# Attention in plain float32 with the two heads of a pair on halves of the TensorE array, instead of a split into high and low parts

## The chip, the cores and the metric

The kernel runs on one core of one Trainium2 chip. The metric is the device time of the program in microseconds (us); the times shown are of separate executions, and one further execution was taken with the hardware profiler. All rows and windows below are of that profiled execution, and times in them count from its first instruction.

## The reference, cut to what matters

Two parts, in float32. First an attention with a memory term, for 4 batches, 8 heads, 576 positions and 64 dimensions per head:

```
scores = q @ k.T / 8, causal mask
a      = softmax(scores)
local  = a @ v
phi(x) = x + 1 where x > 0, else exp(x)
mem    = (phi(q) @ M_prev) / (phi(q) @ z_prev + 1e-6)
out    = g * mem + (1 - g) * local        with g = sigmoid(beta) per head
```

Then a feed-forward on the 2304 rows of 512 that this gives: `h = x @ w_in` (512 to 2048), `r = relu(h)`, `y = (s * r * r + b) @ w_out` (2048 to 512).

## The kernel before, in words

**Pairs.** The 32 heads are worked in 16 pairs; a pair holds two heads of one batch side by side on the 128 partitions (64 dimensions each). Pairs 0 to 3 are batch 0 (`g < NP` in the code). A head's 576 query rows are cut into five tiles: one of 64 and four of 128 (`QS`, `QW`); tile i sees the keys 0 to `QW[i]`, so its scores are 64, 192, 320, 448 and 576 columns wide, the last one in two halves of 288.

**F32R and its split.** TensorE takes a plain float32 matmul as two MATMUL instructions (two passes), each of which streams its columns at half the speed of an F32R pass. F32R keeps fewer bits of its operands, so the kernel writes a number as a high part H (a rounded copy, made by ScalarE) and a low part L (the rest, made by a subtraction on VectorE or GpSimd) and sums several F32R products. The feed-forward does so everywhere (lines L482 to L484 for the first product `mm1`, L745 to L747 for the second).

**Scores.** For pairs 1 to 15 the q and k of a pair are split (`split_qk`, cast L235, subtractions L232 into tile `sqk`) and stacked by four DMAs per pair (`stack_qk`, L269) into `X`, in which a head's high and low parts lie one above the other on 128 partitions. `s_mm` then does two F32R passes per score tile and head (L300, L301). Pair 0 alone takes plain float32 on its 64 partitions (L295). Each tile is masked, scaled and its row minimum taken out of PSUM by one VectorE instruction (`s_red`, L314), then exponentiated with row sums by ScalarE (`s_exp`, L322). `s_norm` makes the reciprocal of the five row sums (L329, L330) and scales the five probability tiles (L334, most on GpSimd), once per head.

**Transposes and the second product.** The probabilities of a head are transposed in 15 blocks by TensorE (`pt_bank`, L373; ten of 128 x 128, four of 128 queries by the first 64 keys, one of 64 by 64) into PSUM banks and copied out by ScalarE. phi(q), scaled by g over its norm (`phi_a` to `phi_c`, L201 to L217), is transposed on its own, two heads at once in five blocks (`t_phi`, L252). For pairs 0 to 3 everything is then multiplied in plain float32 for one head at a time: `av_mm32` with phi by M_prev (L405) and the first 64 keys (L406) on 64 partitions each, and the other keys on 128 (L408). For pairs 4 to 15 (`own`) the transposed probabilities and phi are split as well (`evac`: cast L221, subtraction out of PSUM L225), V is split (`split_v`, L287, L288), the phi parts are stacked by DMA (`stack_qp`), and `av_mm` does F32R passes (L420 to L424) whose output is 128 wide: one half from V's high part, the other from its low part; `av_evac` adds the two (L439, L440). At the end `x_split` splits the pair's output into `xs` (L451 on GpSimd, L452), the operand of `mm1`.

**Order.** Every step has a position in a list `EV` (pair n starts at 2n, head x at x). The list is sorted and run; with it the feed-forward's weights are loaded, converted from 64-bit words and split at positions `WT` (`split_w`, L82 to L85, L470, L471: 16 blocks), and from position 9.75 on the tasks of `mm1` (six F32R passes each, for batches 0 to 2) are spread between the attention's steps; what is left of `mm1` comes after them together with the preparation of `w_out`, and the second product after that. The tile framework plans each engine's order from this one, by its own model of durations; `pin` keeps some instructions in program order. A buffer of a pool is given out again when all readers of its last tile are done. PSUM's eight banks are 2 for scores (`ps_s`), 5 for transposes and `mm1` (`ps_t`) and 1 for the second product (`ps_o`).

## Time and profile before

| what | us |
|---|---|
| median of 3 runs | 662.55 |
| lowest and highest of them | 660.64, 663.14 |
| profiled execution, its own time | 658.63 |
| its span, first to last instruction | 656.5 |

| engine | busy us of the span | instructions |
|---|---|---|
| TensorE, matmuls (PE) | 625.7 | 4536 |
| TensorE, weight loads (PEld) | 572.1 | 4536 |
| VectorE (DVE) | 472.1 | 1109 |
| ScalarE (ACT) | 468.8 | 1053 |
| GpSimd (POOL) | 362.3 | 370 |

Matmuls are pipelined: the duration of one runs to the end of its pipeline and overlaps the next, so busy time of PE is not the work that it does, and what a pass costs is read from start to start. In the rows, `x8` is a count, `<-` stands between what is written and what is read (or between an idle time and what ended it), and `64*128` ahead of a shape is the part of the array used: 64 rows (partitions of the operands) by 128 columns.

### The profile page before, as it was taken

What the parts mean: (1) busy time and instruction counts of PE and PEld (TensorE: products, weight loads), DVE (VectorE), ACT (ScalarE), POOL (GpSimd) and SP (SyncE); (2) the same over time, 40 slices, a digit from 0 to 9 for tenths busy, and PEclk for the clock granted to TensorE, in tenths of its full rate; (3) what the DMA queues carried; (4) which work ended last, traced back from release to release, by engine and by line L of the source; (5) the groups of instructions that cost most, each with busy time, mean ns of one, the idle gap of its engine ahead of it and who ended that gap; (6) DMA issues with size and microseconds to landing.
All of it is one profiled execution on the core that took longest, in us unless ns stands there. A gap on an engine that the chain in (4) does not pass through costs nothing.

```text
span 656.5 us, 13035 instructions
## 1 busy us (share of the span) xinstructions
PE 625.7 (95%) x4536; PEld 572.1 (87%) x4536; DVE 472.1 (72%) x1109; ACT 468.8 (71%) x1053; POOL 362.3 (55%) x370
## 2 busy tenths in 40 slices
PE   5988999979999999999999999999899999999998
PEld 3555566879999999998998999999899999999997
DVE  4987879888767757766867552995967776666781
ACT  5675787767686768757767653769688878898860
POOL 1644777457555755654755431000377678777762
PEclk9997999999999999999999999999989999999999
DMA  7986779587787787786875554657553534543300
GB/s 267 289 226 161 192 202 202 183 199 193 190 217 199 203 209 205 187 219 171 203 202 130 149 199 161 208 181 274 191 159 110 161 92 147 158 141 110 95 34 33
DMA packets 73442, 115.75 MB, mean 176 GB/s; under 512 B 10016, under 2 KB 51232, under 8 KB 73376
## 3 DMA queue, kind: packets, MB, share of 16 engines
q1 hardware_dynamic: 71200, 112.55, 61.0%
q10 hardware_dynamic: 2176, 2.36, 1.0%
q8 instruction: 36, 0.59, 0.4%
q14 instruction: 30, 0.25, 0.1%
HBM read 57.68 MB, written 23.59 MB: 124 GB/s over the span
## 4 chain that ended last, share of the span: by engine, by line
PE 69%; DMA 9%; DVE 6%; ACT 6%; POOL 5%; issue 4%; SPq 1%; POOLq 0%; DVEq 0%; ACTq 0%
PE yps L747 9%; PE yps L745 9%; PE yps L746 9%; PE hps L482 7%; PE hps L483 7%; PE hps L484 7%; PE tps L373 6%; DMA X<-sqk 4%; POOL P L334 4%; PE sps L300 3%; PE sps L301 2%; PE ops L424 2%; PE ops L423 2%; PE tps L252 2%; PE ops L408 1%
## 5 line engine op out<-in xcount | busy, mean ns | idle before, releaser
L334 POOL TENSOR_SCALAR P<-P,sm,omg 128x64 f32<-128x64 f32 (+4 forms) x136 | 98.2, 734 | 61.8 <-DVE sm L330 36.9
L322 ACT ACTIVATE P<-P,mn 128x64 f32<-128x64 f32 (+4 forms) x160 | 89.5, 560 | 39.2 <-DVE mn L314 38.8
L747 PE MATMUL yps<-bH,op 128*128 128x256 f32 x360 | 101.8, 283 | 2.0 <-DVE op L737 2.0
L745 PE MATMUL yps<-bH,op 128*128 128x256 f32 x360 | 101.9, 283 | 1.2 <-ACT r L491 1.2
L746 PE MATMUL yps<-bL,op 128*128 128x256 f32 x360 | 101.8, 283 | 0.0
L314 DVE CUSTOM_DVE_ANT_0 P<-sps,mask 128x64 f32<-128x64 f32 (+4 forms) x160 | 65.9, 423 | 25.9 <-PE sps L301 17.4
L373 PE MATMUL tps<-ident,P 128*128 128x128 f32 (+2 forms) x480 | 75.9, 280 | 6.8 <-POOL P L334 4.6
L482 PE MATMUL hps<-xs,w0H 128*128 128x320 f32 (+1 forms) x256 | 78.4, 306 | 0.4 <-ACT r L491 0.3
L482 PE MATMUL hps<-xs,w1H 128*128 128x320 f32 (+1 forms) x256 | 77.7, 304 | 0.6 <-DVE ptl L225 0.5
L483 PE MATMUL hps<-xs,w0H 128*128 128x320 f32 (+1 forms) x256 | 75.9, 296 | 0.1
L484 PE MATMUL hps<-xs,w0L 128*128 128x320 f32 (+1 forms) x256 | 75.9, 297 | 0.0
L484 PE MATMUL hps<-xs,w1L 128*128 128x320 f32 (+1 forms) x256 | 75.8, 296 | 0.0
L483 PE MATMUL hps<-xs,w1H 128*128 128x320 f32 (+1 forms) x256 | 75.7, 296 | 0.0
L373 PEld LDWEIGHTS tps<-ident,P 128*128 128x128 f32 (+2 forms) x480 | 55.6, 134 | 17.6 <-POOL P L334 7.0
L747 PEld LDWEIGHTS yps<-bH,op 128*128 128x128 f32 x360 | 68.6, 191 | 2.2 <-DVE op L737 2.2
L745 PEld LDWEIGHTS yps<-bH,op 128*128 128x128 f32 x360 | 68.5, 190 | 1.4 <-ACT r L491 1.4
L746 PEld LDWEIGHTS yps<-bL,op 128*128 128x128 f32 x360 | 68.6, 190 | 0.0
L491 ACT ACTIVATE r<-hps 128x320 f32<-128x320 f32 (+1 forms) x128 | 50.5, 408 | 23.9 <-PE hps L484 15.6
L300 PE MATMUL sps<-X 128*128 128x192 f32 (+1 forms) x180 | 60.1, 337 | 5.3 <-DVE mn L314 5.2
L731 POOL TENSOR_TENSOR sum<-w0L 128x512 f32<-128x512 f32 x11 | 18.4, 1677 | 70.6 <-ACT w0L L714 48.2
L301 PE MATMUL sps<-X 128*128 128x192 f32 (+1 forms) x180 | 54.0, 305 | 0.0
L737 POOL TENSOR_TENSOR op<-w0L,op 128x512 fp32r<-128x512 f32 x30 | 43.4, 1464 | 16.4 <-ACT op L736 16.2
(136 smaller groups left out, 1913.7 us busy)
## 6 DMA issues: line engine op xcount, KB each, us to landing
X<-sqk SPq DMA_DIRECT2D x60, 432.0 KB, 5.9
r_d<-r SPq DMA_DIRECT2D x28, 320.0 KB, 3.8
qks<-in_qk_t_dram SPq DMA_DIRECT2D x15, 576.0 KB, 4.7
xa<-in_moe_w_in_dram SPq DMA_DIRECT2D x16, 512.0 KB, 4.9
raw<-in_moe_w_out_dram SPq DMA_DIRECT2D x16, 512.0 KB, 5.0
w1L<-r_d SPq DMA_DIRECT2D x16, 512.0 KB, 4.3
r_d<-r SPq DMA_DIRECT2D x28, 256.0 KB, 3.4
Q<-sqp SPq DMA_DIRECT2D x48, 144.0 KB, 4.2
```

The costliest lines, as they stand in the source:

```text
L300: nc.tensor.matmul(ps[:, :m], lhsT=lhsT, rhs=X[:, 1, c0:c0 + m], start=True, stop=False)
L301: nc.tensor.matmul(ps[:, :m], lhsT=lhsT, rhs=X[:, 2, c0:c0 + m], start=False, stop=True)
L314: nc.vector.tensor_tensor_reduce(P[:, PO[i] + c0:PO[i] + c0 + n], ps[:, :n], mask[:, mo:mo + n], -SCALE, init, ALU.add, ALU.min, mn[:, o:o ...
L322: nc.scalar.activation(pt, pt, AF.Exp, scale=-1.0, bias=mn[:, o:o + 1], accum_out=sm[:, i:i + 1])
L334: dve("nm", x // 2, i).tensor_scalar(pt, pt, sm[:, i:i + 1], omg[:, h:h + 1], ALU.mult, ALU.mult)
L373: nc.tensor.transpose(ps[0:kn, o:o + qn], P[0:qn, c:c + kn], ident[0:qn, 0:qn])
L482: nc.tensor.matmul(ps, lhsT=wH[:, p, fs], rhs=xs[:, 0], start=p == 0, stop=False)
L483: nc.tensor.matmul(ps, lhsT=wH[:, p, fs], rhs=xs[:, 1], start=False, stop=False)
L484: nc.tensor.matmul(ps, lhsT=wL[:, p, fs], rhs=xs[:, 0], start=False, stop=p == NP - 1)
L745: nc.tensor.matmul(ps, lhsT=H, rhs=BH, start=f == 0, stop=False)
L746: nc.tensor.matmul(ps, lhsT=H, rhs=BL, start=False, stop=False)
L747: nc.tensor.matmul(ps, lhsT=L, rhs=BH, start=False, stop=f == KF - 1)
```

## The change: what it does

1. The split of the attention goes: `split_qk`, `stack_qk`, `stack_qp`, `split_v`, `evac`, the F32R branch of the scores and of the second product, and `av_evac` are deleted, with their DMAs. All pairs are worked in plain float32, and a step handles both heads.
2. Scores (`t_score`): four groups per pair (`SCORES`), each with a PSUM bank per head. Per score tile, head 0's matmul is placed on array rows 0 to 63 and head 1's on rows 64 to 127.
3. phi(q) is written by the new `phi_d` into the probability tile `P`, 64 columns ahead of the probabilities of the same query tile, and the transpose of the block with the first 64 keys takes those 64 columns with it (128 columns instead of 64). `t_phi` goes. M_prev and the first 64 rows of V are loaded into one 128-row operand (three DMAs for V instead of one).
4. Second product (`t_av`): per column range, three (lo) or five (hi) steps; in each, head 0 on array columns 0 to 63 and head 1 on columns 64 to 127, into one PSUM bank. `x_split` reads the bank itself: the high part by ScalarE, the low part by VectorE.
5. `s_norm` runs once per pair, after the exponentials of both heads, in the tile order 3, 1, 4, 2, 0; for pairs 4 to 15 the 320 wide tile is on VectorE as before.
6. `P`, the transposed tiles, `qk` and `qs` have two buffers each; PSUM is 3 banks for scores, 4 for transposes and `mm1`, 1 for the second product. Positions are new (`AT`, and `AT0` for pairs 0 to 3); `mm1` starts at 9.97.

```diff
+SCORES = (((3, 0, 448), (0, 0, 64)), ((2, 0, 320), (1, 0, 192)), ((4, 0, 288),), ((4, 288, 288),))
+BANKS = (
+    ((1, 3), (2, 3), (3, 3), (1, 1)),
+    ((1, 4), (2, 4), (3, 4), (1, 2)),
+    ((2, 2), (4, 4), (0, 3), (0, 4)),
+    ((0, 0), (0, 1), (0, 2)),
+)
+AT = dict(
+    qk=-3.0, z=-2.3, q=-2.3, phi_a=-1.5, phi_b=-1.3, phi_c=-0.9, phi_d=-0.3, v=-0.5,
+    score=(0.02, 0.45, 0.95, 1.35), bank=(2.3, 2.55, 2.8, 3.05), av=(3.3, 3.45),
+)
+AT0 = AT | dict(z=-2.99, q=-2.9, phi_a=-2.2, phi_b=-2.0, phi_c=-1.6, phi_d=-1.55)
...
-    ps_s = pa.enter_context(tc.tile_pool(name="ps_s", bufs=2, space=PSUM))
-    ps_t = pa.enter_context(tc.tile_pool(name="ps_t", bufs=5, space=PSUM))
+    ps_s = pa.enter_context(tc.tile_pool(name="ps_s", bufs=3, space=PSUM))
+    ps_t = pa.enter_context(tc.tile_pool(name="ps_t", bufs=4, space=PSUM))
...
+        nc.sync.dma_start(t[0:64, 0], vm[b, p][0:64, 0])
+        nc.sync.dma_start(t[64:128, 0], vm[b, p][64:128, 1])
+        nc.sync.dma_start(t[:, 1:], vm[b, p][:, 2:])
...
+    def phi_d(g):
+
+        p, n, P = st["q", g], st["n", g], probs(g)
+        eng = nc.vector if g < NP else nc.gpsimd
+        for a, w, ts in ((0, 640, slice(2, 5)), (384, 768, slice(1, None, -1))):
+            o = P[:, :, a:].rearrange("q j (t c) -> q t j c", c=w)[:, :, :, 0:64]
+            eng.tensor_mul(o, p[:, ts], n[:, ts].to_broadcast(list(o.shape)))
...
+    def s_norm(g):
+
+        P, sm = st["P", g], st["sm", g]
+        nc.vector.tensor_scalar(sm, sm, 1e-9, None, ALU.add)
+        nc.vector.reciprocal(sm, sm)
+        for i in (3, 1, 4, 2, 0):
+            for j in range(2):
+                h = 2 * (g % NP) + j
+                pt = P[:, j, PB[i] + 64:PB[i] + 64 + QW[i]]
+                eng = nc.vector if g >= NP and i == 2 else nc.gpsimd
+                eng.tensor_scalar(pt, pt, sm[:, j, i:i + 1], omg[:, h:h + 1], ALU.mult, ALU.mult)
+
+    def t_score(g, group):
+        probs(g)
+        qk = st["qk", g]
+        ps = [ps_s.tile([128, 512], F32, tag="s", name="sps") for _ in range(2)]
+        o = 0
+        for i, c0, n in group:
+            for j in range(2):
+                rs = slice(64 * j, 64 * j + 64)
+                nc.tensor.matmul(ps[j][:, o:o + n], lhsT=qk[rs, 0, QS[i]:QS[i] + 128], rhs=qk[rs, 1, c0:c0 + n],
+                                 start=True, stop=True, tile_position=(64 * j, 0))
+            o += n
...
+    def t_bank(g, j, k):
...
+        for kt, i in BANKS[k]:
             qn = 128 if i else 64
+            c = PB[i] + (64 + QS[kt] if kt else 0)
+            nc.tensor.transpose(ps[:, o:o + qn], P[0:qn, j, c:c + 128], ident[0:qn, 0:qn])
             o += qn
+        if k < 2:
+            nc.scalar.copy(pt[:, 0:4, 128 * k:128 * k + 128], ps.rearrange("p (r c) -> p r c", c=128))
+        elif k == 2:
+            nc.scalar.copy(pt[:, 4], ps[:, 0:256])
+            nc.scalar.copy(F[:, 320:576], ps[:, 256:512])
+        else:
+            nc.scalar.copy(F[:, 0:320], ps[:, 0:320])
...
+    def t_av(g, hi):
+
+        ps = ps_o.tile([128, 512], F32, tag="o", name="ops")
+        q0, n = CO[hi], CW[hi]
+        V = st["V", g]
+        steps = []
+        for j in range(2):
+            F, pt = st["F", g, j], st["pt", g, j]
+            steps.append([(V[:, 0, j], F[:, q0:q0 + n], 0)] + (
+                [(V[:, 1 + r, j], pt[:, r], 0) for r in range(3)] + [(V[:, 4, j], pt[:, 4, 128:], 128)] if hi else
+                [(V[:, 1, j], pt[:, 3], 64), (V[:, 2, j], pt[:, 4, :128], 192)]))
+        for k, both in enumerate(zip(*steps)):
+            for j, (lhsT, rhs, o) in enumerate(both):
+                nc.tensor.matmul(ps[64 * j:64 * j + 64, o:n], lhsT=lhsT, rhs=rhs, start=k == 0,
+                                 stop=k == len(steps[0]) - 1, tile_position=(0, 64 * j))
+        later(1, x_split, g, hi, ps[:, :n])
+
+    def x_split(g, c, ps):
...
+        nc.scalar.copy(xs[:, 0], ps)
+        nc.vector.tensor_sub(xs[:, 1], ps, xs[:, 0].bitcast(F32))
```

## Rows read from the trace of the kernel before

**Rows 1.** Busy time in stretches: engine, busy us (instructions); then PEclk, DMA share, GB/s.

```profile
16.00:113.00 97.00, 88.48 (x426) 55.06 (x427) 83.68 (x220) 69.41 (x185) 63.37 (x73) 0.96 0.81 213
113.00:144.00 31.00, 26.62 (x187) 23.56 (x187) 25.42 (x64) 20.16 (x54) 18.33 (x21) 1.00 0.68 184
160.00:384.00 224.00, 219.76 (x1652) 209.25 (x1652) 157.22 (x471) 163.84 (x448) 129.56 (x157) 1.00 0.72 188
```

The columns of Rows 1 are the stretch, its length, then PE, PEld, DVE, ACT and POOL.

**Rows 2.** Timeline of PE, 113.0 to 113.6: start us, us, instruction (the first of `mm1`).

```profile
113.12 0.33 PE L482 MATMUL hps<-xs,w0H 128*128 128x320 f32 x1
```

**Rows 3.** Groups by line and form, DVE, 0 to 113: count | busy us, mean ns.

```profile
L232 DVE TENSOR_TENSOR sqk<-qks,sqk 128x576 fp32r<-128x576 f32 x8 | 6.5, 836 | 2.6 <-ACT sqk L235 2.6
L314 DVE CUSTOM_DVE_ANT_0 P<-sps,mask 128x448 f32<-128x448 f32 x10 | 6.1, 615 | 1.2 <-PE sps L301 1.2
...
L329 DVE TENSOR_SCALAR sm<-sm 128x5 f32<-128x5 f32 x9 | 2.4, 265 | 0.8 <-ACT P L322 0.8
...
L225 DVE TENSOR_TENSOR ptl<-tps,pth 128x512 fp32r<-128x512 f32 x1 | 0.7, 680 | 0.0
```

**Rows 4.** Waits of DVE, 16 to 113: us in total, times, longest.

```profile
DVE P L314 <- PE sps L301: 4.8, 7, 1.8
...
DVE P L314 <- PE tps L373: 2.2, 2, 2.0
```

**Rows 5.** Groups by line and form, PE, 160 to 384.

```profile
L482 PE MATMUL hps<-xs,w0H 128*128 128x256 f32 x74 | 21.8, 295 | 0.0
...
L482 PE MATMUL hps<-xs,w0H 128*128 128x320 f32 x64 | 20.7, 323 | 0.0
...
L373 PE MATMUL tps<-ident,P 64*64 64x64 f32 x19 | 4.6, 243 | 0.0
```

**Rows 6.** Timeline of PE, 183.5 to 184.1.

```profile
183.62 0.37 PE L300 MATMUL sps<-X 128*128 128x448 f32 x1
183.83 0.36 PE L301 MATMUL sps<-X 128*128 128x448 f32 x1
184.03 0.28 PE L483 MATMUL hps<-xs,w1H 128*128 128x256 f32 x1
```

**Rows 7.** Timeline of PE, 186.0 to 187.4.

```profile
186.07 0.27 PE L373 MATMUL tps<-ident,P 128*128 128x128 f32 x1
186.28 0.64 PE L252 MATMUL tps<-ident,qs 64*128 64x64 f32 x3
186.75 0.60 PE L373 MATMUL tps<-ident,P 128*128 128x128 f32 x4
187.11 0.36 PE L482 MATMUL hps<-xs,w1H 128*128 128x256 f32 x1
187.31 0.30 PE L300 MATMUL sps<-X 128*128 128x288 f32 x1
```

A row with a count starts with the first of its instructions and shows that one's shape.

**Rows 8.** Timeline of PE, 176.4 to 177.2.

```profile
176.41 0.55 PE L373 MATMUL tps<-ident,P 128*128 128x128 f32 x3
176.89 0.41 PE L482 MATMUL hps<-xs,w1H 128*128 128x320 f32 x1
177.14 0.31 PE L483 MATMUL hps<-xs,w1H 128*128 128x320 f32 x1
```

**Rows 9.** Timeline of PE, 104.5 to 111.5 (a head of pair 3).

```profile
105.15 0.64 PE L405 MATMUL ops<-sqp,V 64*64 64x256 f32 x2
...
107.81 0.40 PE L300 MATMUL sps<-X 128*128 128x288 f32 x1
...
108.97 0.75 PE L405 MATMUL ops<-sqp,V 64*64 64x320 f32 x2
...
110.98 0.64 PE L252 MATMUL tps<-ident,qs 64*128 64x64 f32 x3
```

**Rows 10.** Timeline of PE, 17.10 to 17.20.

```profile
16.84 0.73 PE L295 MATMUL sps<-qk 64*128 64x320 f32 x1
16.97 0.34 PE L252 MATMUL tps<-ident,qs 64*128 64x64 f32 x1
```

More of the change, by code (lines that the diff above doesn't have):

```diff
@@ new lines, in t_score @@
+    def t_score(g, group):
[9 more added lines that the diff above has]
+            o += n
+        o = 0
+        for i, c0, n in group:
+            for j in range(2):
+                s_red(g, j, i, c0, n, ps[j][:, o:o + n])
+                if c0 + n == QW[i]:
+                    later(1, s_exp, g, j, i)
+            o += n
+        if group == SCORES[-1]:
+            later(2, s_norm, g)
@@ L366, in pt_bank @@
+    def t_bank(g, j, k):
+        P = st["P", g]
+        if ("F", g, j) not in st:
+            st["F", g, j] = ap2.tile([128, S], F32, tag=f"F{j}", name=f"F{j}")
+            st["pt", g, j] = ap2.tile([128, 5, 256], F32, tag=f"pt{j}", name=f"pt{j}")
+        F, pt = st["F", g, j], st["pt", g, j]
         ps = ps_t.tile([128, 512], F32, tag="t", name="tps")
         o = 0
-        runs = []
-        for j, i in blocks:
-            kn = 128 if j else 64
+        for kt, i in BANKS[k]:
             qn = 128 if i else 64
-            c = PO[i] + QS[j]
-            nc.tensor.transpose(ps[0:kn, o:o + qn], P[0:qn, c:c + kn], ident[0:qn, 0:qn])
-            if j == 0:
-                if runs and runs[-1][0] == "k0":
-                    runs[-1][2] += qn
-                else:
-                    runs.append(["k0", QS[i], qn, o])
-            else:
-                half = 1 if i in (2, 4) else 0
-                if runs and runs[-1][0] == half and runs[-1][1] + runs[-1][2] == ROW[j, i]:
-                    runs[-1][2] += 1
-                else:
-                    runs.append([half, ROW[j, i], 1, o])
-            o += qn
@@ L442, in x_split @@
-    def x_split(g, c):
-        x = st.pop(("x", g, c))
-        n, g = g, JOBS[g][0]
+        V = st["V", g]
+        steps = []
+        for j in range(2):
+            F, pt = st["F", g, j], st["pt", g, j]
+            steps.append([(V[:, 0, j], F[:, q0:q0 + n], 0)] + (
[5 more added lines that the diff above has]
+                                 stop=k == len(steps[0]) - 1, tile_position=(0, 64 * j))
@@ L514, in flush @@
             tick()
-    def t_score(x, i, c0=0, n=None):
-        n = n or QW[i]
-        if i == JOBS[x // 2][1][0]:
-            st["P", x] = ap2.tile([128, 1600], F32, tag="P", name="P")
-            st["mn", x] = ap2.tile([128, 6], F32, tag="mn", name="mn")
-            st["sm", x] = ap2.tile([128, 5], F32, tag="sm", name="sm")
-        ps = s_mm(x, i, c0, n)
-        s_red(x, i, c0, n, ps)
-        if c0 + n == QW[i]:
-            later(1, s_exp, x, i)
-            if i == JOBS[x // 2][1][-1]:
-                later(2, s_norm, x)
-    def t_av(x, hi):
-        ps = av_mm(x, hi)
-        later(1, av_evac, x, hi, ps)
-        if x % 2:
-            later(2, x_split, x // 2, hi)
-    if ROUNDS == 2:
-        MM = [(0, c, f, half) for c in range(2) for f in range(NF) for half in range(2)]
-    else:
-        MM = [(0, c, f, half) for fg in range(4) for c in range(2)
-              for f in range(NF // 4 * fg, NF // 4 * fg + NF // 4) for half in range(2)]
+    MM = [(0, c, f, half) for fg in range(4) for c in range(2)
+          for f in range(NF // 4 * fg, NF // 4 * fg + NF // 4) for half in range(2)]
     MM += [(b, c, f, half) for b in range(1, B) for fg in range(2) for c in range(2)
@@ L594, in attention_moe_kernel @@
-    for n, first, last in MMT:
-        for i in range(2 * n):
-            pos = first + (i + 0.5) * (last - first) / (2 * n)
+    for n in range(NPAIR):
+        t = AT0 if n < NP else AT
+        for k, fn in (("qk", load_qk), ("z", load_z), ("q", load_q), ("phi_a", phi_a), ("phi_b", phi_b),
+                      ("phi_c", phi_c), ("phi_d", phi_d), ("v", load_v)):
+            at(2 * n + t[k], fn, n)
+        for pos, group in zip(t["score"], SCORES):
+            at(2 * n + pos, t_score, n, group)
+        for k, pos in enumerate(t["bank"]):
+            for j in range(2):
+                at(2 * n + pos + 0.1 * j, t_bank, n, j, k)
+        for c in range(2):
+            at(2 * n + t["av"][1 - c], t_av, n, c)
@@ L597, in attention_moe_kernel @@
+    for first, last in zip(MMT, MMT[1:]):
+        for i in range(4 * NF):
+            pos = first + (i + 0.5) * (last - first) / (4 * NF)
             if pos < END:
```

293 lines of the change are left out of this document (33 added, 260 removed).

## The prediction

> **What bounds the kernel now.** I read the busy time by stretches first. It shows two regimes and a boundary between them. From 16 to 113 us VectorE is busy 83.7 of 97.0 us and nothing else comes near a full load that counts (PE's 88.5 are overlapping durations) [rows 1]; at 113.12 the first pass of mm1 starts [rows 2]. From 160 to 384 PE is busy 219.8 of 224 us with VectorE at 157, ScalarE at 164, GpSimd at 130 [rows 1]: there, and through the rest of mm1 and the second product, which the change leaves alone, TensorE's own work is the time. So the change has two prices: what it takes from VectorE before 113, and what it does to PE's work per pair after it.
>
> To read PE's work I take starts, not durations. Two F32R passes of 448 columns take 184.03 - 183.62 = 0.41 us, 0.46 ns a column [rows 6]. Four plain float32 transposes of 128 and one F32R pass of 256 take 187.31 - 186.75 = 0.56, less 0.12 for the pass: 0.11 each, 0.86 ns a column [rows 7]. A plain matmul is two such passes, 1.72 ns a column.
>
> Check of the steady stretch: mm1 has twelve forms, six of 256 columns (413 passes in all, the first has 74) and six of 320 (64 each) [rows 5]; 413 x 0.12 + 384 x 0.147 = 106 us. The other 118 us are attention. The 64 x 64 transpose comes once per head and 19 times [rows 5], so it is 9.5 pairs: **12.4 us of PE per pair** before.
>
> **The change, part by part.**
>
> *Do the halves overlap?* One place in the trace of before has two plain float32 instructions on different row halves next to each other: the last score pass of pair 0's second head (320 columns, partitions 64 to 127) starts at 16.84, and the first phi transpose (partitions 0 to 63) at 16.97 [rows 10]. A plain pass of 320 columns needs 320 x 0.86 = 0.28 us at least, so the second did start inside the first: row halves run side by side. No row has two column halves. The instructions stay in order, and of a matmul's two passes the second needs the first to be through; so in a chain A, B, A', B' the second pass of A runs beside the first of B, and a chain costs one pass at its start and two per step, for both heads.
>
> *Scores*: passes of 0.385, 0.055, 0.275, 0.165 and 0.248 us for 448, 64, 320, 192 and 288 columns. Groups: 0.385 + 2 x 0.44 = 1.27; 0.275 + 2 x 0.44 = 1.16; twice 3 x 0.248 = 0.74. Sum 3.91 us a pair. *Second product*: lo has steps of 320, 256, 128: 0.275 + 2 x 0.605 = 1.49; hi four of 256 and one of 128: 0.22 + 2 x 0.99 = 2.20. Sum 3.69. *Transposes*: 28 blocks of 0.11 and two of 0.055: 3.19; the phi transposes go. Total 10.8.
>
> *Change of the array's shape.* Of the transposes from 186.07 to 186.75, one uses 64 rows: 448 columns in 0.68 us, where 448 x 0.86 is 0.39: going into another shape and back costs 0.30 [rows 7]. Around a 64 x 64 transpose: 0.73 for 320 plain columns (0.28) and a pass of 320 (0.15), so 0.31 [rows 8]. Before has three such places a pair in the steady stretch (already in the 12.4). After has eight: four score groups, two of the second product, two transposes of 64 queries. I take 0.30 for each, 2.4; bounds 1.5 (places that fall next to one another share a change) and 4 (the planner puts something between the parts of a group).
>
> The Trainium skill (TensorEngine Tiling, Key Properties) says that a change of the tiling mode drains TensorE and a change of tile inside a mode doesn't. The rows above bear out the first half; of the second there is only rows 10. If each change from half to half cost the same 0.15 as half of such a place, the 22 of a pair would add some 3 us: that is part of the second rival's ground.
>
> *Steady sum*: 10.8 + 2.4 = 13.2, and 0.1 for waits, against 12.4 (in which a few tenths are waits): +0.95 a pair. After the boundary come 11 pairs and pair 4 without its scores (ten heads' score tiles are done by 113 [rows 3]), 11.6 pairs: **+11 us**. VectorE, ScalarE and GpSimd lose work here (all of L225, L232, L288, L440), which gives nothing while PE is the bound. The removed stacking DMAs are off this path too.
>
> *Before the boundary* VectorE loses: eight subtractions of q and k, 6.5 us; the first subtraction of a transposed bank of pair 4, 0.7; half of the nine row-sum steps (one per pair now), 1.2 [rows 3]. It gains nothing: phi_d writes what L217 wrote, x_split's subtraction was there. Sum 8.4 us off the bounding engine. It is idle 97.0 - 83.7 = 13.3 us, 7.0 of them waiting for PE's scores or for a PSUM bank behind a transpose [rows 4]. PE has less to do here: the second product of a head takes 107.81 - 105.15 = 2.66 and 110.98 - 108.97 = 2.01 [rows 9], 9.3 us a pair, against 3.69 + 0.6. Bounds for the waits are none and all of 7; I take 4, so 12.4 in all: the first mm1 at about 101. What is late next is pair 3's chain: normalisation on GpSimd, eight banks on ScalarE, t_av. s_norm now waits for both heads' exponentials and then runs ten scalings; behind it on GpSimd stand the weights' high parts (L470), for which VectorE's L471 waits. The P buffers carry that: the next pair's scores go to the other one.
>
> From 113 to 144 VectorE is still at 25.4 of 31.0 and PE idle for 4.4 [rows 1]; without the work of L225 I count 3 of these back (bounds 0 and 4.4).
>
> *Three loads for V instead of one*, four stacking DMAs fewer per pair: SP's queue gets shorter; nothing, bounds -1 and +1. *Two buffers for qk, P, F and pt*: phi_d of pair n waits for the last bank of pair n-2; on VectorE that wait would stand ahead of the reductions of pair n-1. The planner orders by its own durations, so 0, at worst 5 us before the boundary. *PSUM*: a score group needs two of three banks, so the next one waits for half of the reductions of the last; VectorE's pace is already the bound there. In the steady stretch groups lie some 5 us apart and their reductions take at most 2.
>
> **Sum**: -12.4 - 3 + 11 = -4.4 us on the profiled execution's 658.6 (span 656.5 and 2.1 around it): 654. The median of the runs is 662.6, 3.9 above that execution; with the same 4.4 off it is **658**.
>
> **Rivals.**
>
> 1. *Faster: the changes of shape are cheap or shared.* At 1.5 instead of 2.4 a pair the steady sum is even with before (+0.05 x 11.6), and the stage before the boundary gives all its waits (15.4). Together about -18: 645. For it: the planner already lays score passes directly beside other steps [rows 7]; against: groups are spaced out by their positions, and mm1 stands between.
>
> 2. *Slower: the column halves don't overlap* (or drain at each change). Then the second product costs 4 x 1856 columns x 0.86 ns = 6.4 instead of 3.69, +2.7 a pair, over 11.6 pairs +31: 689. It decides once more than 0.4 us a pair of the overlap is lost. For it: no row shows column halves beside each other; against: the row halves do it [rows 10]. With the row halves failing as well (5.5 instead of 3.91) it is 708.
>
> By the Trainium skill (TensorE: Matmul & The Clock Gate, Measured speedup vs the span model) three column tiles of 32 gave 2.38 times the rate; no run here shows it. An estimate by that page, 0.79 per tile and so 1.6 for two, is 4.0 for the second product where I have 3.69: 662 in place of 658.
>
> 3. *Slower: the order tears the pairs of heads apart.* The plan takes PE's instructions as their banks and operands come ready; head 1's bank may be free later than head 0's, with mm1 passes put between. Each torn group loses its overlap (about 0.3) and pays one more change (0.3): 0.6 x 11.6 = 7 us for each of the six. Half of them torn: 679. For it: three banks for groups of two; against: with VectorE lighter, banks come free early.
>
> 4. *The boundary doesn't move*: the chain of a whole pair (both heads' sums, ten scalings, eight banks) takes the place of VectorE's load as the bound, and only the steady part's price stays: 662.6 + 11 - 3 = 670.
>
> That the change doesn't do what it says has no room in the diff: all pairs go one way.
>
> **How the numbers follow.** A measurement of this kernel can tell 0.5%, 3.3 us, from no change. Forecast 0.46, with a range of its own from 650 to 667 (half of it faster than 659.2, two fifths the same); rival 1: 0.21; rival 2: 0.10; rival 3: 0.12; rival 4: 0.11. Faster: 0.24 + 0.21, and a little of rival 3 with a shorter first stage: 0.46. The same: 0.18 + 0.02. Slower: 0.34. The range leaves out rival 2, the far part of rival 3 and the best of rival 1: 641 to 682.
>
> **What would show each step.** In the trace after: the second passes of one head starting together with the first passes of the other (starts a few ns apart) in t_score and t_av; the first mm1 near 101; PE's time per pair from 160 to 360, worked out as above, near 13.3; six places a pair where a shape changes, each 0.3. The forecast is wrong if the two heads' passes start one full pass apart, if the first mm1 stays near 113, or if a pair costs under 12.4 or over 15 of PE.

## The result, and the profile after

The changed kernel takes 645.53 us (median of 4 runs, 643.07 to 647.12) against 662.47 for the kernel before on the same chip: ratio 0.9745, interval 0.9707 to 0.9783, 2.5% faster. Forecast were 658 and a range of 641 to 682. The profiled execution took 646.29 (span 644.5) where before's took 658.63 (span 656.5). The medians differ by 16.9 and the profiled executions by 12.3: the one shown of before lies 3.8 below its median, the one of after 0.8 above. The working below is of the profiled pair.

Where the 12.0 us of span went, by the times at which the first and the last pass of a product start:

| stretch | before | after | difference | forecast |
|---|---|---|---|---|
| start to first mm1 | 113.1 | 98.7 | -14.4 | -12.4 |
| first to last mm1 | 355.2 | 360.7 | +5.4 | +11 - 3 |
| gap to the second feed-forward product | 1.4 | 1.0 | -0.5 | 0 |
| second feed-forward product | 183.3 | 180.8 | -2.5 | 0 |

The first two rows meet at a place that moves. The first pass of mm1 needs the output of pairs 0 and 1 alone. In before, all 160 passes of the second product of pairs 0 to 3 start ahead of it; in after 98 of 128 do, and the other 30 of pair 3 (some 3.4 us at the upper clock) come behind it, while the scores of about one head more start ahead of it. So a few us of the -14.4 are not saved but have moved into the row below.

First the busy times of after in stretches (columns as in [rows 1]: stretch, length, PE, PEld, DVE, ACT, POOL, granted clock, DMA share, GB/s), which answer to [rows 1].

```profile
16.00:98.70 82.70, 77.81 (x331) 45.87 (x330) 68.09 (x195) 56.54 (x156) 55.97 (x65) 0.90 0.45 140
46.00:80.00 34.00, 31.59 (x194) 19.53 (x190) 30.87 (x95) 28.34 (x85) 25.78 (x29) 1.00 0.40 125
80.00:97.00 17.00, 16.48 (x51) 9.69 (x51) 13.46 (x31) 6.87 (x14) 17.00 (x20) 0.50 0.44 128
160.00:360.00 200.00, 200.00 (x1399) 159.41 (x1398) 70.47 (x275) 116.18 (x336) 60.13 (x86) 1.00 0.29 88
```

Two things are to be seen. In the steady stretch PE has no idle time at all, the busy shares of VectorE and GpSimd have fallen by half, that of ScalarE by a fifth, and the DMA engines go from 0.72 to 0.29. Ahead of mm1 VectorE is almost as full as it was (68.1 of 82.7; it was 83.7 of 97.0), and for 17 us PE runs at half clock, 1.2 GHz, while it is busy for 16.5 of them. [Rows 1] have 0.96 for this stage. The column reads 1.00 up to 46 us in after as well, but the passes there run at the lower level too (last section).

The timeline of PE in after: the first pass of mm1 (which answers to [rows 2]); a hi chain of the second product that is whole and the pass behind it; a lo chain with the mm1 passes around it; two heads' score passes ahead of a transpose; and another hi chain, whose first matmul (217.54) runs alone, ahead of the rest (219.72). Columns: start, us, instruction, count.

```profile
98.68 0.42 PE L327 MATMUL hps<-xs,w0H 128*128 128x320 f32 x1
...
170.82 0.65 PE L291 MATMUL ops<-F,V 128*64 128x256 f32 x4
171.31 1.68 PE L291 MATMUL ops<-pt,V 128*64 128x256 f32 x16
172.92 0.42 PE L327 MATMUL hps<-xs,w1H 128*128 128x320 f32 x1
...
177.29 0.28 PE L327 MATMUL hps<-xs,w1H 128*128 128x256 f32 x1
177.50 0.76 PE L291 MATMUL ops<-F,V 128*64 128x320 f32 x4
178.09 0.82 PE L291 MATMUL ops<-pt,V 128*64 128x256 f32 x8
178.84 0.39 PE L328 MATMUL hps<-xs,w1H 128*128 128x256 f32 x1
179.07 0.28 PE L329 MATMUL hps<-xs,w1L 128*128 128x256 f32 x1
...
210.90 1.23 PE L239 MATMUL sps<-qk 64*128 64x288 f32 x6
212.06 0.33 PE L265 MATMUL tps<-ident,P 128*128 128x128 f32 x1
...
217.54 0.65 PE L291 MATMUL ops<-F,V 128*64 128x256 f32 x2
218.12 0.59 PE L239 MATMUL sps<-qk 64*128 64x192 f32 x2
...
219.72 0.43 PE L291 MATMUL ops<-F,V 128*64 128x256 f32 x1
```

The rows with counts unfold, from start to start, into this (columns of a pass : ns to the next start):

```
177.50  320:6 320:314 320:6 320:263 256:6 256:210 256:6 256:209 128:7 128:103 128:6 128:203
210.90  288:6 288:340 288:7 288:236 288:242 288:334
```

The first line is the overlap: two passes start 6 ns apart, then nothing for the length of one. The second line is a torn group: the first two matmuls are a pair of heads in this way, the last two passes, 242 and 334 ns, are one head alone. Hi chains are torn as well. Only 2 of the 13 from 98 us on are whole (20 passes in 2.10 us, as at 170.82). In the others one head's first matmul runs alone, 0.58 us as at 217.54, and the other 18 passes start some 1.5 to 3.4 us later and take 2.09 all the same.

The groups of PE from 160 to 360 in after (count | busy us, mean ns | idle), which answer to [rows 5]:

```profile
L327 PE MATMUL hps<-xs,w0H 128*128 128x320 f32 x64 | 21.0, 329 | 0.0
...
L327 PE MATMUL hps<-xs,w0H 128*128 128x256 f32 x40 | 12.5, 313 | 0.0
...
L265 PE MATMUL tps<-ident,P 64*128 64x64 f32 x16 | 4.0, 252 | 0.0
```

The 64 x 64 transpose comes sixteen times, so this is eight pairs. Over all forms mm1 has 312 passes of 256 columns and 379 of 320: 312 x 0.12 + 379 x 0.147 = 93.2 us. The other 106.8 us are **13.36 us per pair**, where the forecast had 13.2 and 0.1 for waits, and before has 12.4 with its waits.

Waits of VectorE in after, 16 to 98.7 (us in total, times, longest), which answer to [rows 4]; then those of PE in the same stretch.

```profile
DVE w0L L316 <- POOL w0H L315: 4.2, 4, 2.1
DVE P L195 <- PE tps L265: 3.5, 1, 3.5
DVE P L209 <- PE tps L265: 2.9, 1, 2.9
```

```profile
PE sps L239 <- DVE mn L209: 3.2, 4, 1.7
PE tps L265 <- POOL P L228: 2.4, 5, 0.7
```

VectorE now waits for GpSimd's part of the weights (L315) and once 3.5 us with `phi_d` (L195) for the probability buffer that PE is still transposing: the wait that the prediction named as a risk. PE waits for 5.6 us of 82.7. The same view of before gives it 9.1 of 97:

```profile
PE tps L373 <- POOL P L334: 3.4, 4, 1.4
PE ops L405 <- ACT x L435: 2.5, 2, 1.6
PE sps L300 <- DVE mn L314: 2.3, 3, 1.1
```

These are its three largest; the other two are 0.7 and 0.2. So PE had little slack ahead of mm1 as well, in both kernels; in before VectorE, idle for 97.0 - 83.7 = 13.3 us [rows 1], had somewhat more. From start to start, waits included, PE's 97 us of before are 40.6 second product, 32.6 scores, 18.9 transposes and 4.9 phi transposes; its 82.7 of after are 14.8, 40.8 and 26.9. The second product gave 26 back (in part because 30 of its passes now come later), and scores and transposes took 11 of them again. The lower clock accounts for those: in e10 below, where it reads 1.00 from 46 us on, scores take 32.7 and transposes 24.0, about what they took in before.

### The profile page after: what moved, and what is told of

Same layout as the page of the kernel before. It is cut to its first block, busy times and chain, and to the rows that moved or that the text cites. A ratio compares the mean times of both kernels' runs of the same rounds, so it can differ in the third digit from the quotient of the medians.

```text
span 644.5 us, 12039 instructions
## 1 busy us (share of the span) xinstructions
PE 627.1 (97%) x4424; PEld 531.0 (82%) x4424; DVE 366.4 (57%) x895; ACT 420.0 (65%) x950; POOL 274.8 (43%) x286
## 4 chain that ended last, share of the span: by engine, by line
PE 73%; issue 13%; POOL 6%; DVE 5%; DMA 2%; ACT 1%; SPq 0%; POOLq 0%; ACTq 0%
PE sps L239 10%; PE yps L548 9%; PE yps L546 9%; PE yps L547 9%; PE tps L265 9%; PE hps L327 7%; PE ops L291 7%; PE hps L328 6%; PE hps L329 6%; POOL P L228 5%; DMA qs<-in_q_rows_dram 2%; DVE P L209 1%; DVE w1H L490 1%; DVE op L538 0%; POOL sum L532 0%
## 5 line engine op out<-in xcount | busy, mean ns | idle before, releaser
L228 POOL TENSOR_SCALAR P<-P,sm,omg 128x448 f32<-128x448 f32 (+4 forms) x136 | 98.4, 739 | 113.7 <-DVE sm L222 96.4
L216 ACT ACTIVATE P<-P,mn 128x448 f32<-128x448 f32 (+4 forms) x160 | 88.7, 557 | 35.9 <-DVE mn L209 35.9
L239 PE MATMUL sps<-qk 64*128 64x288 f32 (+4 forms) x384 | 100.4, 479 | 10.5 <-DVE mn L209 5.8
L209 DVE CUSTOM_DVE_ANT_0 P<-sps,mask 128x448 f32<-128x448 f32 (+4 forms) x160 | 60.8, 424 | 54.9 <-PE sps L239 48.6
L239 PEld LDWEIGHTS sps<-qk 64*128 64x128 f32 x384 | 52.9, 211 | 42.5 <-issue 18.4
L265 PE MATMUL tps<-ident,P 128*128 128x128 f32 (+1 forms) x480 | 83.9, 297 | 2.6 <-POOL P L228 2.4
L265 PEld LDWEIGHTS tps<-ident,P 128*128 128x128 f32 (+1 forms) x480 | 57.9, 149 | 29.7 <-issue 15.4
L327 PE MATMUL hps<-xs,w0H 128*128 128x320 f32 (+1 forms) x256 | 79.9, 313 | 0.0
L328 PE MATMUL hps<-xs,w0H 128*128 128x320 f32 (+1 forms) x256 | 76.3, 298 | 0.0
L532 POOL TENSOR_TENSOR sum<-w0L 128x512 f32<-128x512 f32 x11 | 16.5, 1497 | 96.4 <-ACT w0L L515 75.4
L327 PEld LDWEIGHTS hps<-xs,w0H 128*128 128x128 f32 x256 | 48.3, 189 | 6.8 <-issue 4.1
```

What stands on the lines that cost most here:

```text
L209: nc.vector.tensor_tensor_reduce(P[:, at0:at0 + n], ps, mask[:, mo:mo + n], -SCALE, init, ALU.add, ALU.min, mn[:, o:o + 1])
L216: nc.scalar.activation(pt, pt, AF.Exp, scale=-1.0, bias=mn[:, o:o + 1], accum_out=sm[:, i:i + 1])
L228: eng.tensor_scalar(pt, pt, sm[:, j, i:i + 1], omg[:, h:h + 1], ALU.mult, ALU.mult)
L239: nc.tensor.matmul(ps[j][:, o:o + n], lhsT=qk[rs, 0, QS[i]:QS[i] + 128], rhs=qk[rs, 1, c0:c0 + n], start=True, stop=True, tile_position=(6 ...
L265: nc.tensor.transpose(ps[:, o:o + qn], P[0:qn, j, c:c + 128], ident[0:qn, 0:qn])
L327: nc.tensor.matmul(ps, lhsT=wH[:, p, fs], rhs=xs[:, 0], start=p == 0, stop=False)
```

## The experiments

Ratios are to the kernel before in the same job; after itself has 0.9745, and 0.9746 in a second job. "Paired" is the share of passes that start within 20 ns of the other head's, from first mm1 on: in after 61% of the score passes and 85% of the second product's. A pass that starts inside a longer one of the other head counts as alone, so the share is a lower bound of the overlap. The mm1 stretch is the time from the first to the last pass of mm1, and a stop is a place in it where PE goes over to score passes from something else.

A ratio says nothing of where in the kernel a difference lies. By the same cuts as above, in the profiled execution of each run (us):

| run | ratio | start to first mm1 | first to last mm1 | second feed-forward product |
|---|---|---|---|---|
| before | 1 | 113.1 | 355.2 | 183.3 |
| after, two jobs | 0.9745, 0.9746 | 98.7, 98.9 | 360.7, 360.7 | 180.8, 181.1 |
| e1, second product's heads apart | 1.0063 | 93.2 | 388.8 | 181.5 |
| e2, heads in turn inside a score group | 0.9825 | 102.5 | 363.5 | 181.2 |
| e13, score groups apart | 1.0034 | 99.5 | 376.1 | 181.1 |
| e4, four score banks | 0.9597 | 94.9 | 355.7 | 183.2 |
| e8, four banks, groups in close pairs | 0.9659 | 93.8 | 360.1 | 180.7 |
| e3, wide transposes | 0.9684 | 94.2 | 361.7 | 181.8 |
| e9, four banks and wide transposes | 0.9564 | 89.6 | 355.0 | 181.2 |
| e5, more work for VectorE | 0.9641 | 97.8 | 362.9 | 181.4 |
| e6, before with plain scores | 1.002 | 117.0 | 360.4 | 182.9 |
| e7, more work for PE | 0.9841 | 102.2 | 363.3 | 181.1 |
| e10, e1 for pairs 0 to 3 alone | 0.9776 | 94.5 | 363.2 | 181.1 |

e5 and e7 change nothing behind the first mm1, and their middle column is still 2 to 3 us from that of after. Differences of that size in one column show nothing by themselves.

### Do the column halves overlap? (rival 2)

```diff
-        for k, both in enumerate(zip(*steps)):
-            for j, (lhsT, rhs, o) in enumerate(both):
+        for j, own in enumerate(steps):
+            for k, (lhsT, rhs, o) in enumerate(own):
```

> The changed kernel, with the second product's matmuls in the order of all steps of head 0, then all of head 1, on the same column halves. If the column halves truly overlap and TensorE's work is the bound after the first mm1, the second product costs 4 x 1856 columns x 0.86 ns = 6.4 us a pair instead of 3.9, +2.5 over some 11.6 pairs: about +29 us, 674. If the overlap is worth little (TensorE waits for others there anyway), under +5: 650. The first mm1 stays near 99 in either case.

Measured: ratio 1.0063 [1.0036, 1.0089], 669.32 us. PE in this kernel, a lo chain from its first pass to the mm1 pass behind it:

```profile
178.49 0.75 PE L291 MATMUL ops<-F,V 128*64 128x320 f32 x2
179.08 0.38 PE L291 MATMUL ops<-pt,V 128*64 128x256 f32 x1
...
180.42 0.39 PE L329 MATMUL hps<-xs,w1L 128*128 128x256 f32 x1
```

1.93 us instead of 1.34, with the same twelve passes; only the end of one head and the start of the other interleave (13% paired). Over the mm1 stretch the second product takes 72.6 us by starts instead of 50.3, and the stretch is 388.8 long instead of 360.7. That 28 is close to the +29 expected, but 22 of it is the second product; the rest stands at scores (3.3), mm1 (1.6) and transposes (0.9). The total shows less because the first mm1 came 5.5 earlier (93.2). The overlap of the column halves is real, and without it the change would gain nothing: its price in the mm1 stretch would be near rival 2's +31. That the boundary came *earlier* with more work on PE was not expected; in this kernel the granted clock is 1.00 in the stretch where after has 0.50:

```profile
43.00:93.20 50.20, 49.40 (x274) 31.84 (x272) 43.86 (x129) 38.00 (x108) 37.31 (x45) 1.00 0.42 123
```

### Do the row halves overlap, and what does tearing cost? (rival 3)

Order of the passes inside a score group, one head after the other:

```diff
-        for i, c0, n in group:
-            for j in range(2):
+        for j in range(2):
+            o = 0
+            for i, c0, n in group:
...
```

> The changed kernel, with each score group's matmuls in the order of head 0's, then head 1's. If pairing of the row halves is what keeps the scores at 4.4 us a pair, losing the two thirds that run paired costs about 1.2 us a pair: +14, 659. If the pairing is mostly torn already by other causes, or hidden, under +4: 649.

Measured: 0.9825 [0.9779, 0.9871], 652.7 us; first mm1 102.5, scores in the mm1 stretch 49.1 instead of 47.6 us. Half of the groups have one tile per head, which this edit leaves as they were, and in the others the end of one head still meets the start of the next: 52% of the passes stay paired. It tells little.

Groups taken apart into a step per head, 0.2 of a position apart, with one bank each:

```diff
-            at(2 * n + pos, t_score, n, group)
+            for j in range(2):
+                at(2 * n + pos + 0.2 * j, t_score, n, group, j)
...
```

> The changed kernel with each score group as two steps, head 0's and, 0.2 positions later, head 1's, each with one bank. Changing the order inside a group left 52% of the score passes after the first mm1 paired (61% before), so it said little on the row halves. If row halves side by side are worth what column halves are, unpaired scores cost 5.5 us of passes a pair instead of 4.4 with waits, and some three more changes of shape: +2.0 x 11.6 = 23 us, ratio 1.01. If the pairing of the scores matters little, under +5 us: ratio 0.975 to 0.982.

Measured: 1.0034 [1.0, 1.0067], 663.75. The score steps of one pair's heads now stand apart in PE's timeline:

```profile
183.98 1.13 PE L239 MATMUL sps<-qk 64*128 64x320 f32 x4
185.04 0.39 PE L327 MATMUL hps<-xs,w1H 128*128 128x256 f32 x1
...
187.11 0.80 PE L239 MATMUL sps<-qk 64*128 64x320 f32 x2
```

Scores in the mm1 stretch take 60.4 us (+12.8), stops at score steps rise from 55 to 70, and the paired share falls to 30%. That is +19 us in total for half of the pairing lost, near the +23 expected. Of the 12.8, fifteen more stops at 0.3 make some 4.5 (an estimate, by the price in [rows 7]); the rest, some 8, is passes that ran alone. So the row halves overlap too, and pairing them pays; that they are worth just what the column halves are is not shown.

Then the other way: four banks for scores, three for transposes and mm1.

```diff
-    ps_s = pa.enter_context(tc.tile_pool(name="ps_s", bufs=3, space=PSUM))
-    ps_t = pa.enter_context(tc.tile_pool(name="ps_t", bufs=4, space=PSUM))
+    ps_s = pa.enter_context(tc.tile_pool(name="ps_s", bufs=4, space=PSUM))
+    ps_t = pa.enter_context(tc.tile_pool(name="ps_t", bufs=3, space=PSUM))
```

> The changed kernel with four PSUM banks for scores and three for transposes and mm1. In the changed kernel a third of the score passes run alone, not beside the other head's. If that is for want of a second free bank, four banks pair them: about -0.9 for the passes and -0.3 for a change of shape less, per pair, over 11.6 pairs -14: 632. If they are torn for another reason it stays at 645; if three banks are too few for transposes and mm1, it gets slower, to 650 or 660.

Measured: 0.9597 [0.9554, 0.964], 637.9: 1.5% below after. A score group of this kernel and the transpose behind it, PE's timeline:

```profile
200.40 0.76 PE L239 MATMUL sps<-qk 64*128 64x288 f32 x4
201.09 0.66 PE L265 MATMUL tps<-ident,P 128*128 128x128 f32 x4
```

A whole group of four passes of 288 takes 0.69 with both heads in it. Stops 34 instead of 55, paired 72%, scores 43.4 us instead of 47.6. So rival 3 was at work in after, and want of banks is part of it: with three, 39% of the score passes ran alone, with four still 28%. By the medians the kernel gains some 11 us (0.9745 x 665.7 - 637.9, the median of before in this job being 665.7), where 14 were expected. But of the 6.7 between the profiled executions only 4.9 lie in the mm1 stretch, where all 14 were expected; 3.8 lie ahead of the first mm1, and the second feed-forward product takes 2.5 back. So what four banks add to the pairing of the scores is worth far less than expected.

Four banks, and the four groups issued as two close pairs:

```diff
-    score=(0.02, 0.45, 0.95, 1.35), ...
+    score=(0.02, 0.03, 0.95, 0.96), ...
```

> The kernel with four score banks, and the four score groups of a pair placed in two pairs of neighbours (positions 0.02, 0.03, 0.95, 0.96). With four banks TensorE went to scores 34 times after the first mm1, 2.9 times a pair. If each change of shape costs 0.3 us, two stops a pair save another 0.3 x 0.9 x 11.6 = 3 us: 0.5% less than with four banks alone. If VectorE's reductions of a group (2 us) then hold up the next, TensorE waits or the groups are torn again: the same or slower by up to 1%.

Measured: 0.9659 [0.9599, 0.9719], 641.02 us; 37 stops against 34 of the four banks alone, paired 61%, scores 48.1 us. The second branch of the expectation came: no fewer stops, and groups torn again. That the second group waits for banks of the first, which VectorE has still to read, is the likely reason; no run shows it.

### Changes of the array's shape (rival 1)

The transpose of the tile of 64 queries uses 64 rows and brings two changes per pair. Made 128 wide, it writes 64 columns more, over which the next block writes:

```diff
-            nc.tensor.transpose(ps[:, o:o + qn], P[0:qn, j, c:c + 128], ident[0:qn, 0:qn])
-            o += qn
+            nc.tensor.transpose(ps[:, o:o + 128], P[:, j, c:c + 128], ident)
+            o += 128 if i else 64
```

> The changed kernel, with the two transposes of 64 queries per pair made 128 wide, so that they don't change the array's shape (64 more columns each, 0.055 us). If a change of shape and back costs 0.3 us of TensorE's time where it is the bound, -0.6 + 0.1 a pair: -6 us, 640. If these places are hidden behind waits, or what costs there is something else, 0: 645.

Measured: 0.9684 [0.9643, 0.9724], 644.01, 0.6% below after by the ratios, whose intervals overlap. Transposes in the mm1 stretch take 41.1 us instead of 44.8: 3.7 over 12 pairs is 0.31 a pair, while two places at 0.30, less 0.055 more for each of two wider transposes, would be 0.5. But scores took 1.7 more (49.3), mm1's passes 2.4 and the second product 0.6, so that the stretch is 361.7 long, not shorter than the 360.7 of after. The 6 us expected there did not come; the profiled execution is shorter because its first mm1 came 4.5 earlier (94.2), and why it did was not settled. So this run doesn't decide rival 1. The timeline of after does: around the lo chain at 177.50 the mm1 pass ahead takes 0.21 instead of 0.12 and the one behind 0.223, and the chain itself 1.34 where its passes need 704 x 2 x 0.86 ns = 1.21. That is 0.32 for going in and out, the full price.

Both edits that helped, together (four banks and the wide transpose), in one job with a second run of after:

> Four score banks together with the transposes of 64 queries made 128 wide. Alone they gave ratios to the kernel before of 0.960 and 0.968, where the changed kernel has 0.9745. If both take changes of shape from TensorE where it is the bound, they add: 0.953 to 0.955, some 10 us under the changed kernel's 645. If they work on the same waits, 0.960.

> The changed kernel once more, beside the next two on one chip, for the comparison with them and for how much its first stage varies: first mm1 between 94 and 100, depending on how long the clock stays at its lower level before it; ratio to the kernel before 0.97 to 0.978.

Measured: 0.9564 [0.9532, 0.9596], 631.85, against 0.9746 [0.971, 0.9782], 643.99. The two intervals lie apart: 1.9% below after, 4.4% below before. PE's first mm1 and busy times of this kernel:

```profile
89.61 0.41 PE L326 MATMUL hps<-xs,w0H 128*128 128x320 f32 x1
```

```profile
160.00:360.00 200.00, 200.00 (x1446) 162.93 (x1445) 68.22 (x266) 116.31 (x334) 60.43 (x86) 1.00 0.28 87
```

In the same 200 us PE runs 1446 instructions instead of 1399, without idle time. The ratios nearly add up: 1.5% and 0.6% alone, 1.9% together. But of the 15.8 us between the two profiled executions 9.3 lie ahead of the first mm1 (89.6 against 98.9) and 5.7 in the mm1 stretch. Both edits were meant for the second place; why they help more in the first was not settled.

### What sets the first mm1?

The prediction's bound was VectorE's load. Eight extra subtractions on VectorE, of the kind removed (into a tile nobody reads), for pairs 1 to 4:

```diff
+        if 1 <= n <= NP:
+            at(2 * n - 1.4, extra, n, 0)
+            at(2 * n - 1.38, extra, n, 1)
```

> The changed kernel with eight VectorE subtractions of 128 x 576 added for pairs 1 to 4 (into a tile that nobody reads), at the positions where the kernel before had its eight subtractions of q and k: 6.5 us of VectorE. If VectorE's load still sets when the first mm1 starts, it moves from 98.7 to about 105 and the time is 1.0% longer than the changed kernel's. If the chain through GpSimd's scalings, or TensorE at its lower clock level, has taken over that stage, the first mm1 moves by under 2 us.

The extra group of VectorE, 0 to 98, and PE's first mm1:

```profile
L164 DVE TENSOR_TENSOR scr<-qk 128x576 f32<-128x576 f32 x8 | 6.0, 746 | 1.9 <-DMA qk<-in_qk_t_dram 1.9
```

```profile
97.76 0.42 PE L332 MATMUL hps<-xs,w0H 128*128 128x320 f32 x1
```

6.0 us more of VectorE and the first mm1 is 0.9 *earlier* (ratio 0.9641 [0.9563, 0.9719]). VectorE's load does not set it in after. The same on before, from the other side: pairs 1 to 3 with plain scores (`NS = 4` instead of 1), so that six of the eight subtractions go and nothing else of the change comes.

> The kernel before with one part of the change alone: the scores of pairs 1 to 3 in plain float32, one head at a time (pair 0 has them so already). It takes six subtractions (5.0 us) from VectorE and twelve stacking DMAs, and gives TensorE some 2 us more per pair. If VectorE's load sets the start of the first mm1, it moves from 113 to about 108 and the time falls by 5 us, 0.75%. If TensorE's work counts as much there, it stays at 113 or gets later.

VectorE's subtractions in this kernel up to 117, and PE's first mm1:

```profile
L232 DVE TENSOR_TENSOR sqk<-qks,sqk 128x576 fp32r<-128x576 f32 x2 | 1.9, 938 | 2.5 <-ACT sqk L235 2.5
```

```profile
116.99 0.39 PE L482 MATMUL hps<-xs,w0H 128*128 128x320 f32 x1 [0.23 <-DVE ptl L225]
```

VectorE has 4.6 us less; PE waits for 4.0 us of this stage instead of 9.1; and the first mm1 comes 3.9 *later* (ratio 1.002 [0.9982, 1.0059]). So in the kernel on which the prediction was built VectorE's load did not set that time alone, and PE's work counted. The edit changes both engines' work and the DMAs at once, so it doesn't show that PE's work alone set it.

Is it then the lower clock? One extra plain matmul of 288 columns on the full array ahead of each score group of pairs 0 to 3:

```diff
+        if g < NP:
+            nc.tensor.matmul(ps[0][:, 0:288], lhsT=ident, rhs=mask[:, 0:288], start=True, stop=True)
```

> The changed kernel with one more plain float32 matmul, full array, 288 columns, ahead of each score group of pairs 0 to 3 (its result is overwritten by the scores): 0.5 us and a change of shape for each of sixteen. With the second product's heads apart, TensorE had more to do before the first mm1, its clock stayed at the upper level from 43 us on, and the first mm1 came 5.5 us earlier. If the lower level of the clock (80 to 97 us in the changed kernel, and up to 46) is what holds that stage, more work for TensorE shortens it: first mm1 near 93, time 0.8% less. If not, the sixteen fillers only delay it: first mm1 at 100 to 110.

Measured: 0.9841 [0.9779, 0.9904], 653.97 us, first mm1 102.2. The granted clock of this kernel:

```profile
21.00:58.50 37.50, 37.14 (x99) 20.86 (x99) 24.13 (x75) 18.31 (x48) 16.17 (x23) 0.50 0.37 117
58.50:102.00 43.50, 42.16 (x246) 25.19 (x244) 35.39 (x107) 34.28 (x99) 27.04 (x32) 1.00 0.40 125
```

PE is fuller (37.1 of 37.5) and still at the lower level up to 58.5. More work for PE did not bring the upper level, and the fillers delayed the stage, as the last branch of the expectation has it. Last, the heads of the second product apart in pairs 0 to 3 alone, since e1 had kept its clock:

```diff
-        for k, both in enumerate(zip(*steps)):
-            for j, (lhsT, rhs, o) in enumerate(both):
+        order = [(k, j) for k in range(len(steps[0])) for j in range(2)]
+        for k, j in sorted(order, key=lambda x: x[1]) if g < NP else order:
+            for lhsT, rhs, o in steps[j][k:k + 1]:
```

> The changed kernel, with the second product's heads one after the other (no overlap of the column halves) for pairs 0 to 3 alone: 2.5 us more of TensorE's work per pair, 10 us, before the first mm1; the steady part is as in the changed kernel. With the heads apart everywhere the first mm1 came 5.5 us earlier, with the clock at the upper level from 43 us on. If the clock's level is the cause, it comes at about 93 here too and the time falls by 5 us, 0.8%. If that was chance, or TensorE's plain amount of work counts, it comes at 99 to 109 and the time is the same or up to 1.5% longer.

```profile
46.00:94.50 48.50, 47.70 (x266) 30.85 (x262) 40.27 (x122) 36.23 (x103) 35.37 (x44) 1.00 0.41 119
```

The clock stays at 1.00 from 46 us to the first mm1, which comes at 94.5, 4.4 earlier than in the run of after beside it (98.9), although the second product of the stage takes 6.7 more: scores take 32.7 instead of 41.2, transposes 24.0 instead of 26.8. So the lower level does cost that stage. The total did not follow: 645.42 (0.9776 [0.9741, 0.981]) against 643.99. Two things take the gain away. The mm1 stretch was 363.2, 2.5 longer, and all of that is the second product (52.8 instead of 50.3): most of pair 3's comes behind the first mm1, with its heads apart. And the profiled execution of after is its slowest in this job. Its three executions at a mean granted clock of 0.995 take 643.3 to 643.8, its two at 0.987 take 646.9 and 647.3: after itself often has those 3.5 us already. The 5 us expected are not there.

## Why the prediction was right in its range, and where its steps failed

The forecast was 4.4 us off a median of 662.6, and 16.9 came: 12.3 in the profiled executions, and 4.6 because the one of before lies below its median and that of after above. Of the 7.6 that the profiled pair gained beyond the forecast's 4.4 (12.0 of span), 2.0 lie ahead of the first mm1, 2.6 between it and the last, 3.0 behind. The range held; the time is that of rival 1.

- **Overlap of the halves: right.** It rested on one place in before, of row halves only [rows 10]. In after the passes of two heads start 6 to 7 ns apart in both steps; losing the one costs 22 us of PE time in the mm1 stretch (e1), losing half of the other 13, more stops included (e13). The lo chain at 177.50 and the hi chain at 170.82 take 1.34 and 2.10 us, where 6.38 were worked out without overlap: 1.86 times; with a torn hi chain (2.09 and 0.58) it is 1.59. So the estimate worked out from a figure of the Trainium skill (TensorE: Matmul & The Clock Gate, Measured speedup vs the span model), 1.6 for two tiles, was too careful for whole chains and near for torn ones.
- **"A chain costs one pass at its start": wrong, too dear.** The passes do not go A, B, A', B' one behind the other; first passes of both heads run together, then second passes. The forecast has such a lead pass for each of six chains: 0.275 and 0.22 in the second product, 0.385, 0.275 and twice 0.248 in the scores. That is 1.65 a pair too much.
- **Both steps at full overlap: wrong, too cheap.** In after 39% of the score passes run alone, and 11 of 13 hi chains are torn. From 160 to 360 the lone score passes have 18,528 columns: at half of 0.86 ns each that is at most 8.0 us over eight pairs, 1.0 a pair. Seven of the eight hi chains there are torn, 0.5 a pair. So tearing took back about what the lead passes gave, and the steady sum (13.36 measured, 13.3 forecast) was right only as a sum. The forecast put the third bank down as harmless, "VectorE's pace is already the bound there", and gave rival 3 a chance of 0.12; it was in part there. e4 takes some of it out; why the hi chains are torn was not tried.
- **Changes of shape: right in number and price.** From 160 to 360 the shape changes 136 times, 17 a pair, 8.5 places where eight were counted (its list of signs has six), and the place around the chain at 177.50 costs 0.32. That taking two places a pair away pays in the mm1 stretch is not shown (e3).
- **VectorE as the bound before mm1: wrong, the step that failed.** The forecast read 83.7 of 97.0 us as the load that counts, and set PE's 88.5 aside as overlapping durations [rows 1], though PE's waits in before come to no more than 9.1 us. The 8.4 us credited to VectorE's lost work, and the 4 of its 7 for waits [rows 4], were the wrong terms: e5 adds 6.0 to VectorE and e6 takes 4.6 off it, and neither moves the first mm1 the way that theory asks. What came in their place, by PE's starts, is the drop of the second product that the forecast mentions (9.3 against 4.3 us a pair [rows 9]) and does not enter: 26 us of PE, less 11 for scores and transposes at the lower clock. Most of this drop is not the overlap's: by the passes done ahead of the first mm1, a pair's second product takes 10.2 us there in before, 6.5 with the heads apart (e10: 21.6 us for 106 passes of 32 a pair) and 4.8 in after. No run brings the old second product back into after, so this account is a reading of PE's starts and not an experiment. 14.4 came near 12.4 by accident.
- **The stacking DMAs: put at nothing, and nothing speaks against it.** The DMA share fell by more than half in the steady stretch, and PE waits for no DMA there in either kernel. No run takes them away alone.
- **After the boundary: +5.4 instead of +8.** By starts, mm1's passes have 3.8 us more (a pass next to a change is longer), scores 1.4, the second product 0.4, the transposes 0.2 less. The busy times of the stretch, of before and of after:

```profile
113.12:468.37 355.25, 345.73 (x2580) 330.91 (x2579) 253.96 (x692) 253.03 (x652) 170.09 (x200) 1.00 0.69 193
```

```profile
98.68:459.36 360.68, 360.68 (x2562) 300.77 (x2562) 163.87 (x500) 219.85 (x579) 94.06 (x129) 1.00 0.38 120
```

  PE is idle for 9.5 us of it in before and for none in after. So PE's own time grew by about 15 us here, and the waits that went hid 9.5 of it; the forecast had 11 and 3.
- **The second feed-forward product: -2.5, not forecast and left open.** In before PE waits there once 2.0 us for VectorE, and its granted clock is 0.79 from 474 to 482:

```profile
PE yps L747 <- DVE op L737: 2.0, 1, 2.0
```

```profile
474.00:482.00 8.00, 6.03 (x38) 5.82 (x38) 8.00 (x10) 4.36 (x8) 3.33 (x2) 0.79 0.51 169
```

  The profiled execution of e4 has such a place (a wait of 1.9) and takes 183.2 for the product as before does; the other runs of the changed kernel have 180.7 to 181.8. Whether the change moves its likelihood was not tried.

Rival 1 gave the measured time, 645, by a mechanism that is not there: changes cost their full price, and the stretch behind the first mm1 became longer. Rival 4's chain, GpSimd's scaling of the probabilities, does lead the chain of waits up to 100 us (24.7% of it; PE's scores 14.6, transposes 12.3), and GpSimd is busy for all of 80 to 97; yet the boundary moved.

## What to carry to other kernels

Before an engine is called the bound of a stage, look at the waits of *every* engine in it: here PE waited less than the loaded VectorE, and 6 us more work for VectorE did not delay the stage. When two heads share the array by halves, look in the timeline for passes that run alone: groups that need two PSUM banks were torn more often with three banks than with four, and a chain's first matmul can stand alone as well. Cut every run by stage before a gain is put down to an edit: e3 and e9 gained more ahead of the first mm1 than in the stretch that they were made for. A sum that comes out right is no proof of its terms: here one of 1.65 us a pair was cancelled by others of the opposite sign.

## What the runs showed of the hardware

- Two plain float32 matmuls on different halves start 6 to 7 ns apart, pass by pass, and a chain of them needs no lead pass: at 177.50 two heads' passes of 320 columns take 263 to 314 ns together, where one alone is worked out at 275.
- Going into another shape of the array and back costs 0.32 us around the lo chain at 177.50, of which some 0.2 stand at the mm1 passes ahead of it and behind it and not in the chain.
- A stage with paired passes on halves of the array was granted 0.50 (1.2 GHz) with PE busy for 16.5 of 17.0 us, where the same stage with the second product's heads apart kept 1.00 (e1, e10). A full-array matmul more in each score group (e7) did not raise it: 0.50 with PE busy for 37.1 of 37.5. What the level follows from was not settled.
- The granted clock reads 1.00 from 16 to 46 us in after, but the passes tell otherwise: eight transposes starting at 31.62 take 1.90 us to the next start, 0.24 each, where [rows 7] have 0.11. In before the same holds up to 27: fifteen transposes from 22.70 take 3.28 to the next start, 0.22 each. A clock column without a fall in it is to be checked against the pitch of a known pass.

```profile
31.62 1.97 PE L265 MATMUL tps<-ident,P 128*128 128x128 f32 x8
33.52 0.84 PE L239 MATMUL sps<-qk 64*128 64x288 f32 x1
```
